# A denominator reciprocal of 128x512 turned into one of 128x128 between two trips through DRAM, with a small reordering of the setup, in a fused scan and attention kernel

## The chip, the cores and the metric

The kernel runs on one core of one Trainium2 chip. The metric is the device time of the kernel in microseconds (us); where several runs were made, the median. Lower is better. TensorE (PE) multiplies matrices, VectorE (DVE), ScalarE (ACT) and GpSimd (POOL) work elementwise, SyncE (SP) issues most of the DMAs. Each engine takes its instructions in the order in which they were written, and waits on semaphores for the others.

## The reference

Two independent branches share one output of 2048 x 1280, the first 640 columns from A and the others from B.

```python
# A: a diagonal state-space layer
Lam_bar = exp(dt * Lam);  B_bar = ((Lam_bar - 1.0) / Lam)[:, None] * Bmat
Bu = einsum("bld,pd->blp", x, B_bar)          # 2048 x 640, complex
for t in range(L): h = Lam_bar * h + Bu[:, t] # a scan along the sequence
y = 2.0 * einsum("blp,dp->bld", hseq, Cmat).real + x * Dskip
# B: attention with 32 query heads of width 20 and one shared key/value head
scores = einsum("bhqd,bkd->bhqk", q, k) * 20 ** -0.5
p = softmax(scores);  o = einsum("bhqk,bkd->bhqd", p, v) @ wo
```

The softmax divides each query's row by its denominator. The change is about how that division is prepared, and about the order of some setup work.

## The kernel before, in words

**Attention.** The 2048 queries are cut into 4 blocks of 512 (`NQB`), each block's 32 heads into 8 groups of 4 heads (`NGG`), so there are 32 groups. A group has 64 score units, one for each of its 4 heads and each of 16 chunks of 128 keys: 2048 units in all. TensorE writes the transposed scores of 3 or 2 units at a time into a PSUM tile (`R`, ring of two), and ScalarE turns the tile into exponentials in `P` (L1232, tiles of 1536 or 1024 columns in turn). About a fifth of the units goes another way: scores into a bank of `B`, then VectorE makes an approximate exponential by integer arithmetic: one pass out of PSUM (L1237, "eviction") and three shifted copies (L1242, of 1 to 3 units at once). TensorE multiplies all of them with the values and a column of ones, so that `PV` gathers, for each of 4 heads, 20 rows of output and one row of denominators. VectorE copies a finished group to `OTr` (L1275, `raw_op`), and SP stores it to DRAM, `o_rows` (`norm_ops`), 128 rows of 512 queries for each group, 32 rows for each head, with the denominators in row 20 of each 32.

**Denominators.** When all 8 groups of a block are in DRAM, `dense_ops` (L964) reads them back. Four DMAs load the block's 32 rows of denominators into `rwide`, [128, 512], the same 32 rows four times, once for each quarter of the partitions; four more load the outputs into `OTd` with head and dimension laid out densely. VectorE inverts all of `rwide` in one instruction (L982), and GpSimd multiplies `OTd` by it in 20 pieces of 128x128 (L989). Then `proj_ops` multiplies `OTd` by the output weights on TensorE. The 32 different rows of 512 denominators are thus inverted four times over. In the last block the groups 6 and 7 go another way (`norm_last`), and the dense part holds the first six, so that it can start two groups ahead of the end.

**The guard.** A bound on each query's scores is subtracted by an extra contraction row. Its weights `Md` are built in `dense_setup` by GpSimd: a memset, four selects (L600), then five multiplies (L604) with `md`, the key's largest magnitudes, which come back from DRAM (`m_row`) by four DMAs. The first matmuls that use `Md` are those of `qd_block(0)`.

**The scan (A).** `post_constants` computes small constants on GpSimd, with one reciprocal on VectorE (L709), `scan_ops` builds the output weights (`CGre`, `CGim`; GpSimd L845, VectorE L847), and for each of 4 sequence blocks and 5 channel chunks VectorE and GpSimd rotate, scan (L915) and rotate back.

**What sets the order.** `setup` is written out by hand. From then on a planner (`Plan`, `main`) writes the program when the kernel is built: it keeps a clock for each engine, takes the instruction that can begin first (with biases for each thread of work and some noise), and books it with a planned duration (`occ`) and latency (`lat`). `dve_t(n)` is n/960 + 0.07 us; a DMA is booked with at least 0.5 us of issue and 2.5 us to land. How many units go to VectorE comes out of this. `SEEDS` gives one random seed for each 64th of the score units. Each engine, SP with its DMAs too, then runs the fixed list that comes out of the plan, whatever the real durations are.

Of the kernel before, what the change touches and what calls it, by code (L numbers as in the profile page):

```python
# [9 lines left out]
ALU = mybir.AluOpType  # L10
AX = mybir.AxisListType
FP32 = mybir.dt.float32
BF16 = mybir.dt.bfloat16
# [200 lines left out]
def dve_t(n, rate=1.0):  # L214
    return n / (960.0 * rate) + 0.07
# [28 lines left out]
class _Kernel:  # L244
# [17 lines left out]


    TURNS = 64
    SEEDS = (1006, 2008, 3007, 4006, 0, 6002, 7007, 8004, 0, 10002, 11008, 0, 13008, 14008, 15009, 16002, 17007,
# [4 lines left out]

    def __init__(self, nc, t):
        self.nc, self.t = nc, t
# [21 lines left out]
    def alloc(self):  # L294
# [42 lines left out]
        self.part = self.wqd[:].rearrange("p c n -> p (c n)").bitcast(FP32)[:, 0:1280].rearrange("p (t n) -> p t n", t=2)  # L337
        self.sb("rden", [128, 2, 16], BF16)
        self.sb("rwide", [128, 512], BF16)
        self.Qs = nc.dram_tensor("q_rows", (1, 1024, 512), BF16, kind="Internal").ap()  # L340
        self.Os = nc.dram_tensor("o_rows", (self.NQB, 1024, 512), BF16, kind="Internal").ap()
        self.Ms = nc.dram_tensor("m_row", (1, 20), FP32, kind="Internal").ap()
# [236 lines left out]
    def dense_setup(self, pool):  # L579

        K, NC = self, self.NC
        go = self.go
        zero = bass.AP(tensor=K.OTr, offset=512, ap=[[1024, 32], [0, 11], [1, 512]])
        rows = lambda x, o, *ap: bass.AP(tensor=x.tensor, offset=o, ap=[*ap])
        go(self.dma(rows(K.Ms, 0, [1, 20], [1, 1]), K.mabs[0:20, 4:5], "Ms", reads=["mabs"], writes=["Ms"], kb=1))
        go(self.dma(rows(K.Qs, 21 * 512, [32 * 512, 32], [512, 11], [1, 512]), zero, "Qsz", reads=["OTr1"], writes=["Qsz"],
                    kb=352))
        last = self.NQB - 1
        for i in range(2):
            go(self.dma(K.Os[last, 128 * (6 + i):128 * (7 + i), :], K.OTr[:, 1, :], "Osz", reads=["OTr1"],  # L590
                        writes=[f"Os{last}_{6 + i}"], kb=128))
        go(self.dma(rows(K.Os, last * 1024 * 512 + (32 * 24 + 20) * 512, [32 * 512, 8], [1, 512]),
                    bass.AP(tensor=K.WO4, offset=3 * 640, ap=[[(NC + 2) * 640, 1], [0, 8], [1, 512]]), "Oso",
                    reads=["onesrow", f"Os{last}_6", f"Os{last}_7"], writes=[f"Os{last}_6", f"Os{last}_7"], kb=8))
        for dd in range(4):
            go(self.dma(K.md[32 * dd:32 * dd + 32, :], rows(K.Ms, dd, [0, 32], [4, NC]), "md", reads=["Ms"],
                        writes=[f"md{dd}"], kb=1))
        pool(lambda e: e.memset(K.Md[:], 0.0), writes=["Md"])
        for dd in range(4):
            pool(lambda e, dd=dd: e.affine_select(out=K.Md[:], in_=K.Md[:], pattern=[[0, NC], [-1, 32]],  # L600
                                                  compare_op=ALU.not_equal, fill=-1.02, base=-32 * dd, channel_multiplier=1),
                 ["Md"], ["Md"], occ=0.4)
        for m in range(NC):
            pool(lambda e, m=m: e.tensor_scalar(K.Md[:, m, :], K.Md[:, m, :], K.md[:, m:m + 1], None, op0=ALU.mult),  # L604
                 ["Md"] + [f"md{i}" for i in range(4)], ["Md"])

    def v_part(self):
        K, NC = self, self.NC
# [143 lines left out]
    def qd_block(self, qb):  # L752

        K, NC = self, self.NC
        xs = [f"xbT{c}" for c in range(NC)]
        ops, guard = [], []
        gate = lambda: self.units >= 64 * (self.NGG * (qb - 1) + 1)
        for m in range(NC):
            h = Hold()
            for c in range(NC):  # L760
                ops.append(self.mms([self.m1(lambda h=h: h.T[:, :], K.wqd[:, c, 128 * m:128 * m + 128],
                                             K.xbT[:, c, 512 * qb:512 * qb + 512], c == 0, c == NC - 1)],
                                    [f"wqd{c}"] + xs, [None], accum=c > 0, lock=c == 0, gate=gate if c == 0 else None,
                                    hold=h))
            ops.append(Op("dve", lambda e, m=m, h=h: e.tensor_scalar(K.Qd[:, m, :], h.T[:, :], self.c1, None, op0=ALU.mult),
                          [None], [f"Qd{m}"], occ=dve_t(512), free=True, hold=h))
        qd = [f"Qd{m}" for m in range(NC)]
        read = lambda: self.qread >= self.NGG * qb
        for dd in range(4):
            dst = bass.AP(tensor=K.Qs.tensor, offset=dd * 512, ap=[[32 * 512, 32], [4 * 512, NC], [1, 512]])  # L770
            ops.append(self.dma(dst, K.Qd[32 * dd:32 * dd + 32, :, :], "Qs", reads=qd, writes=[f"Qs{dd}"], kb=160,
                                gate=read if dd == 0 else None))
        h = Hold()
        seq = ["a", "a", "g", "a", "g", "a", "g", "a", "g", "g"]
        na = ng = 0
        for x in seq:
            if x == "a":
                ops.append(Op("dve", lambda e, m=na: e.tensor_scalar(
                    K.Qab[:, m % 2, :], K.Qd[:, m, :].bitcast(I16), 0x7FFF, None, op0=ALU.bitwise_and),
                    [f"Qd{na}"], [f"Qa{na % 2}", "Qpos"], occ=dve_t(512, 4), kind="fast"))  # L780
                na += 1
            else:
                ops.append(self.mms([self.m1(lambda: h.T[0:32, :], K.Md[:, ng, :], K.Qab[:, ng % 2, :].bitcast(BF16),
                                             ng == 0, ng == NC - 1, (0, 0))], ["Md", f"Qa{ng % 2}"], [None], accum=ng > 0,
                                    lock=ng == 0, hold=h))
                ng += 1
        ops.append(Op("dve", lambda e: e.tensor_copy(K.Gs[:, :], h.T[0:32, :]), [None], ["Gs"], occ=dve_t(512), free=True,
                      hold=h))
        ops.append(self.dma(bass.AP(tensor=K.Qs.tensor, offset=20 * 512, ap=[[32 * 512, 32], [1, 512]]), K.Gs[:, :], "QsG",
                            reads=["Gs"], writes=["QsG"], kb=32, done=lambda: self.qsent.add(qb)))  # L790
        return ops
# [12 lines left out]
    def scan_ops(self):  # L804
# [34 lines left out]
        for c in range(NC):  # L839
            cr, ci = K.Craw[c][:, 0, :], K.Craw[c][:, 1, :]  # L840
            keys = [f"Craw{c}0", f"Craw{c}1", "sc"] + (["ostage0", "ostage1"] if c == 4 else ws)
            for (dst, x, y, gx, gy, op, nm) in ((K.CGre, cr, ci, GRE, GIM, ALU.subtract, "CGre"),
                                                (K.CGim, ci, cr, NGRE, NGIM, ALU.add, "CGim")):
                for i in range(0, 640, 128):
                    pool(lambda e, y=y, c=c, gy=gy, i=i: e.tensor_scalar(K.ctmp[:, i:i + 128], y[:, i:i + 128], sc[:, gy, c:c + 1],  # L845
                                                                         None, op0=ALU.mult), keys, [f"ct{i}"] + ct * (i == 0), 128)
                dve(lambda e, dst=dst, x=x, op=op, c=c, gx=gx: e.scalar_tensor_tensor(  # L847
                    out=dst[:, c, :], in0=x, scalar=sc[:, gx, c:c + 1], in1=K.ctmp, op0=ALU.mult, op1=op),
                    keys + ct + [f"ct{i}" for i in range(0, 640, 128)], [nm], 640)
        sc_[-1].done = lambda: prog.update(c=1)  # L850
        for b in range(4):
            for c in range(NC):
# [110 lines left out]
    def dense_ops(self, qb):  # L963
# [4 lines left out]
        ops = []  # L968
        have = lambda: all(g in self.normed for g in range(self.NGG * qb, self.NGG * qb + (6 if qb == self.NQB - 1 else 8))) and (
            qb == 0 or qb - 1 in self.projected)  # L970
        for dd in range(4):
            src = bass.AP(tensor=K.Os.tensor, offset=base + 20 * 512, ap=[[32 * 512, 32], [1, 512]])
            ops.append(self.dma(K.rwide[32 * dd:32 * dd + 32, :], src, "rwide", reads=rd, writes=[f"rw{dd}"], kb=32,
                                gate=have if dd == 0 else None))
        for dd in range(4):
            src = bass.AP(tensor=K.Os.tensor, offset=base + dd * 512, ap=[[32 * 512, 32], [4 * 512, NC], [1, 512]])
            ops.append(self.dma(K.OTd[32 * dd:32 * dd + 32, :, :], src, "OTd", reads=rd,
                                writes=[f"OTd{m}{h}" for m in range(NC) for h in self.PIECES] if dd == 0 else [f"OTe{dd}"], kb=160))

        def recip(e):  # L980
            with self.nc.allow_low_precision("bf16 reciprocal of softmax denominator"):
                return e.reciprocal(K.rwide[:], K.rwide[:])  # L982
        rw = [f"rw{dd}" for dd in range(4)]
        ops.append(Op("dve", recip, rw, rw, occ=dve_t(512)))
        n = 512 // len(self.PIECES)
        for i, h in enumerate(self.PIECES):
            c = slice(n * i, n * i + n)
# [507 lines left out]
```

## Time and profile before

| | before |
|---|---|
| median of 3 runs (lowest to highest) | 785.59 us (785.25 to 786.33) |
| the profiled execution | 786.13 us |
| its span, first to last instruction | 784.4 us |
| ScalarE busy | 760.4 us, 97% |
| VectorE busy | 707.0 us, 90% |
| TensorE busy | 686.8 us, 88% |
| GpSimd busy | 440.8 us, 56% |

Durations and moments are those of the profiled execution, counted from the start of its span. A row of a timeline gives start, length, engine, line, operation and tiles; equal instructions that follow each other are merged, with their count behind an x, and an idle time before them stands in square brackets with what ended it. A row of a group gives line, engine, operation, count, busy time, the mean of one, and the idle time before the group with what ended it.

### The profile page before, as it was taken

The page shows a single profiled execution, that of the slowest core. Times are in us where ns is not written, and L with a number is a line of the kernel's source. Part 1 is how long each engine was busy: PE and PEld are TensorE (multiplying, and loading weights), DVE is VectorE, ACT ScalarE, POOL GpSimd, SP SyncE. Part 2 cuts the span into 40 slices and gives each one's busy share as a digit, 9 for nine tenths or more (in the row PEclk, how much of TensorE's full clock was granted, in tenths as well). Part 3 has the DMA queues.
Part 4 walks back from the last instruction along what each step waited for, and adds up shares of the span by engine and source line. Part 5 has one row for each costly group of instructions (what it writes and reads, how often), then busy time and mean ns, then how long its engine had stood idle before and what let it go on. Part 6 is the DMA issues. An engine that isn't in the chain of part 4 may idle for free.

```text
span 784.4 us, 16444 instructions
## 1 busy us (share of the span) xinstructions
PE 686.8 (88%) x6429; PEld 214.1 (27%) x6500; DVE 707.0 (90%) x1206; ACT 760.4 (97%) x688; POOL 440.8 (56%) x865
## 2 busy tenths in 40 slices
PE   5899887888879999988888999888898998889987
PEld 1222222222213233322222223222232332223333
DVE  6599899999988988899997978899999889998896
ACT  7999999999989999999998999999999999999995
POOL 4614854799987111099978300699972339990040
PEclk9799999999999999999999999999999999999999
DMA  8476101000020100220010010310002101000200
GB/s 184 86 148 124 41 15 48 16 15 15 1 55 24 39 16 16 57 58 15 14 48 25 15 39 31 65 34 16 9 23 58 37 24 39 1 14 17 65 10 34
DMA packets 59610, 31.23 MB, mean 40 GB/s; under 512 B 39942, under 2 KB 59534, under 8 KB 59534
## 3 DMA queue, kind: packets, MB, share of 16 engines
q1 hardware_dynamic: 57392, 29.86, 15.7%
q8 instruction: 52, 0.85, 0.5%
q10 hardware_dynamic: 2142, 0.32, 0.2%
q14 instruction: 24, 0.20, 0.1%
HBM read 9.08 MB, written 12.56 MB: 28 GB/s over the span
## 4 chain that ended last, share of the span: by engine, by line
ACT 68%; DVE 16%; PE 8%; POOL 2%; DMA 2%; SPq 2%; issue 1%; POOLq 0%; DVEq 0%
ACT P L1232 68%; DVE Pd L1237 5%; DVE Pd L1242 4%; PE R L418 3%; PE B L418 3%; PE PV L418 2%; DVE rwide L982 2%; DVE hh L915 1%; POOL tm L845 1%; SPq L399 1%; DMA md<-m_row 1%; DVE tm L888 1%; DMA xbT<-in_B_x_dram 1%; POOL uh L904 1%; DMA o_rows<-OTr 0%
## 5 line engine op out<-in xcount | busy, mean ns | idle before, releaser
L1232 ACT ACTIVATE P<-R 128x1536 bf16<-128x1536 f32 (+1 forms) x655 | 742.4, 1418 | 11.3 <-PE B L418 9.3
L418 PE MATMUL R<-QT,KT 32*128 32x512 bf16 (+1 forms) x1636 | 258.1, 388 | 68.3 <-ACT P L1232 47.9
L1237 DVE TENSOR_SCALAR Pd<-B 128x512 int16<-128x512 f32 x412 | 278.4, 682 | 32.2 <-PE B L418 28.4
L1242 DVE TENSOR_SCALAR Pd<-Pd 128x1536 int16<-128x1536 int16 (+2 forms) x501 | 256.8, 546 | 1.2
L418 PE MATMUL PV<-Pd,VP 128*32 128x512 bf16 x1648 | 251.1, 385 | 2.6 <-DVE OTr L1275 1.2
L418 PE MATMUL PV<-P,VP 128*32 128x512 bf16 x1636 | 248.8, 387 | 3.2 <-DVE Pd L1242 2.7
L904 POOL TENSOR_TENSOR tm<-hh,cs 128x128 bf16<-128x128 f32 x320 | 165.6, 540 | 22.9 <-DVE hh L915 10.1
L418 PE MATMUL B<-QT,KT 32*128 32x512 bf16 x412 | 159.5, 387 | 0.0
L418 PEld LDWEIGHTS R<-QT,KT 32*128 32x128 bf16 (+1 forms) x1636 | 64.2, 91 | 305.9 <-ACT P L1232 274.5
L904 POOL TENSOR_TENSOR W<-tm 128x128 bf16<-128x128 bf16 x160 | 89.7, 583 | 97.5 <-PE B L418 93.4
L904 POOL TENSOR_TENSOR uh<-tm 128x128 bf16<-128x128 bf16 x160 | 82.1, 534 | 81.8 <-DVE tm L888 77.4
L418 PEld LDWEIGHTS PV<-Pd,VP 128*32 128x32 bf16 x1648 | 59.5, 94 | 66.4 <-issue 40.9
L418 PEld LDWEIGHTS PV<-P,VP 128*32 128x32 bf16 x1636 | 57.5, 94 | 60.2 <-issue 42.3
L989 POOL TENSOR_TENSOR OTd<-OTd,rwide 128x128 bf16<-128x128 bf16 x80 | 32.7, 436 | 51.4 <-DVE rwide L982 49.5
L888 DVE TENSOR_TENSOR tm<-B,cs 128x1024 bf16<-128x1024 f32 x40 | 48.6, 1214 | 1.7 <-PE B L418 1.2
L418 PE MATMUL B<-CGre,W 128*128 128x384 bf16 (+1 forms) x160 | 46.5, 305 | 0.1
L418 PE MATMUL B<-CGim,W 128*128 128x384 bf16 (+1 forms) x160 | 45.6, 299 | 0.0
L915 DVE TENSOR_TENSOR_SCAN hh<-sc,hini,uh 128x512 f32<-128x512 f32 x30 | 40.4, 1345 | 0.0
L845 POOL TENSOR_SCALAR tm<-W,sc 128x128 f32<-128x128 bf16 x40 | 31.6, 802 | 14.7 <-DVE CGre L847 8.1
L418 PEld LDWEIGHTS B<-QT,KT 32*128 32x128 bf16 x412 | 37.3, 91 | 0.0
L418 PE MATMUL B<-xaT,BTre 128*128 128x512 bf16 x89 | 27.2, 383 | 2.1 <-issue 1.3
L418 PE MATMUL B<-xaT,BTim 128*128 128x512 bf16 x85 | 27.1, 392 | 2.2 <-issue 1.7
(149 smaller groups left out, 416.5 us busy)
## 6 DMA issues: line engine op xcount, KB each, us to landing
o_rows<-OTr SPq DMA_DIRECT2D x32, 128.0 KB, 1.7
QT<-q_rows SPq DMA_DIRECT2D x30, 128.0 KB, 2.2
q_rows<-Qd SPq DMA_DIRECT2D x16, 160.0 KB, 2.8
OTd<-o_rows SPq DMA_DIRECT2D x16, 160.0 KB, 3.4
out_dram<-ystage SPq DMA_DIRECT2D x16, 160.0 KB, 1.8
out_dram<-ostage SPq DMA_DIRECT2D x12, 160.0 KB, 1.8
P<-in_B_wq_dram SPq DMA_DIRECT2D x1, 800.0 KB, 5.4
WO<-in_B_wo_dram SPq DMA_DIRECT2D x4, 200.0 KB, 3.6
```

Source lines behind the costliest of these rows:

```text
L399: return e.dma_start_transpose(out_ap, in_ap)
L418: ins = e.matmul(o() if callable(o) else o, lhsT=l, rhs=r, start=st, stop=sp, skip_group_check=True, **kw)
L845: pool(lambda e, y=y, c=c, gy=gy, i=i: e.tensor_scalar(K.ctmp[:, i:i + 128], y[:, i:i + 128], sc[:, gy, c:c + 1], None, op0=ALU.mult), key ...
L888: dve(lambda e, k=k, h=h: e.tensor_tensor(K.tm[:, 2 * k:2 * k + 2, :], bass.AP(tensor=K.BB, offset=512 * int(h.key[1]), ap=[[512 * self.BA ...
L904: put(lambda e, c0=c0, end=end: e.tensor_tensor(out[:, c0:end], a[:, c0:end], b[:, c0:end], op), reads, [writes + h], n, gate=None if i el ...
L915: dve(lambda e, ri=ri, ini=ini: e.tensor_tensor_scan(K.hh[:, ri, :], dec, K.uh[:, ri, :], ini, ALU.mult, ALU.add), ["sc", *(f"uh{ri}{h}" f ...
L982: return e.reciprocal(K.rwide[:], K.rwide[:])
L989: ops.append(Op("pool", lambda e, c=c, m=m: e.tensor_tensor(K.OTd[:, m, c], K.OTd[:, m, c], K.rwide[:, c], ALU.mult), rw + [f"OTe{dd}" for ...
L1232: return Op("act", lambda e: e.activation(dst, K.R[n % 2][:, 0:512 * size], ACT.Exp, scale=self.exp_scale), [f"R{n % 2}"] + ["R0c"] * (siz ...
L1237: return Op("dve", lambda e: e.tensor_scalar(K.Pd[:, 0, u, :], K.B[x][:, :], self.d_off, 0.0, op0=ALU.add, op1=ALU.max), [f"B{x}"], [f"Pd{ ...
L1242: return Op("dve", lambda e: e.tensor_scalar(K.Pd[:, i, a:b, :], K.Pd[:, 0, a:b, :], float(self.SHIFTS[i]), 0.0, op0=ALU.subtract, op1=ALU ...
```

## The change

The diff has five parts.

1. `dense_ops`: the block's denominators are loaded into a new buffer `rblk`, [128, 128], in four DMAs of 32 rows by 128 columns, so that each denominator is there once, the four column quarters stacked on the partitions. VectorE inverts `rblk` in one instruction. Four DMAs write it back over the denominators in `o_rows`, and four DMAs load the inverted rows into `rwide`, four times over as before. For each block there are 8 more DMAs, all in SP's queue, and `rwide` waits for the stores. GpSimd's multiplies are unchanged, and now wait for the loads of `rwide` where they waited for VectorE.
2. The five multiplies that finish `Md` move from `dense_setup` to `qd_block(0)`, so that the planner places them; they come behind the scan's constants on GpSimd.
3. The planned latency of the `md` DMAs is 5.5 in place of 2.5.
4. The planned duration of the `CGre` and `CGim` instructions is that of 695 columns in place of 640.
5. The seeds are others, so the planner's order differs on every engine.

```diff
@@ -262,11 +262,10 @@
     TURNS = 64
-    SEEDS = (1006, 2008, 3007, 4006, 0, 6002, 7007, 8004, 0, 10002, 11008, 0, 13008, 14008, 15009, 16002, 17007,
...
+    SEEDS = (1006, 2007, 3008, 4004, 5008, 6003, 0, 8008, 9006, 0, 11003, 0, 13002, 14008, 0, 16002, 17003,
...
@@ -337,6 +336,7 @@
         self.part = self.wqd[:].rearrange("p c n -> p (c n)").bitcast(FP32)[:, 0:1280].rearrange("p (t n) -> p t n", t=2)
         self.sb("rden", [128, 2, 16], BF16)
         self.sb("rwide", [128, 512], BF16)
+        self.sb("rblk", [128, 128], BF16)
         self.Qs = nc.dram_tensor("q_rows", (1, 1024, 512), BF16, kind="Internal").ap()
         self.Os = nc.dram_tensor("o_rows", (self.NQB, 1024, 512), BF16, kind="Internal").ap()
         self.Ms = nc.dram_tensor("m_row", (1, 20), FP32, kind="Internal").ap()
@@ -593,16 +593,15 @@
                     bass.AP(tensor=K.WO4, offset=3 * 640, ap=[[(NC + 2) * 640, 1], [0, 8], [1, 512]]), "Oso",
                     reads=["onesrow", f"Os{last}_6", f"Os{last}_7"], writes=[f"Os{last}_6", f"Os{last}_7"], kb=8))
         for dd in range(4):
-            go(self.dma(K.md[32 * dd:32 * dd + 32, :], rows(K.Ms, dd, [0, 32], [4, NC]), "md", reads=["Ms"],
-                        writes=[f"md{dd}"], kb=1))
+            o = self.dma(K.md[32 * dd:32 * dd + 32, :], rows(K.Ms, dd, [0, 32], [4, NC]), "md", reads=["Ms"],
+                         writes=[f"md{dd}"], kb=1)
+            o.lat = 5.5
+            go(o)
         pool(lambda e: e.memset(K.Md[:], 0.0), writes=["Md"])
         for dd in range(4):
             pool(lambda e, dd=dd: e.affine_select(out=K.Md[:], in_=K.Md[:], pattern=[[0, NC], [-1, 32]],
                                                   compare_op=ALU.not_equal, fill=-1.02, base=-32 * dd, channel_multiplier=1),
                  ["Md"], ["Md"], occ=0.4)
-        for m in range(NC):
-            pool(lambda e, m=m: e.tensor_scalar(K.Md[:, m, :], K.Md[:, m, :], K.md[:, m:m + 1], None, op0=ALU.mult),
-                 ["Md"] + [f"md{i}" for i in range(4)], ["Md"])
 
     def v_part(self):
         K, NC = self, self.NC
@@ -771,6 +770,9 @@
             ops.append(self.dma(dst, K.Qd[32 * dd:32 * dd + 32, :, :], "Qs", reads=qd, writes=[f"Qs{dd}"], kb=160,
                                 gate=read if dd == 0 else None))
         h = Hold()
+        if qb == 0:
+            ops.extend(Op("pool", lambda e, m=m: e.tensor_scalar(K.Md[:, m, :], K.Md[:, m, :], K.md[:, m:m + 1], None, op0=ALU.mult),
+                          ["Md"] + [f"md{i}" for i in range(4)], ["Md"], occ=0.25) for m in range(NC))
         seq = ["a", "a", "g", "a", "g", "a", "g", "a", "g", "g"]
         na = ng = 0
         for x in seq:
@@ -846,7 +848,7 @@
                                                                          None, op0=ALU.mult), keys, [f"ct{i}"] + ct * (i == 0), 128)
                 dve(lambda e, dst=dst, x=x, op=op, c=c, gx=gx: e.scalar_tensor_tensor(
                     out=dst[:, c, :], in0=x, scalar=sc[:, gx, c:c + 1], in1=K.ctmp, op0=ALU.mult, op1=op),
-                    keys + ct + [f"ct{i}" for i in range(0, 640, 128)], [nm], 640)
+                    keys + ct + [f"ct{i}" for i in range(0, 640, 128)], [nm], 695)
         sc_[-1].done = lambda: prog.update(c=1)
         for b in range(4):
             for c in range(NC):
@@ -968,20 +970,29 @@
         ops = []
         have = lambda: all(g in self.normed for g in range(self.NGG * qb, self.NGG * qb + (6 if qb == self.NQB - 1 else 8))) and (
             qb == 0 or qb - 1 in self.projected)
+        row = base + 20 * 512
+        den = lambda b: bass.AP(tensor=K.Os.tensor, offset=row + 128 * b, ap=[[32 * 512, 32], [1, 128]])
+        part = lambda b: K.rblk[32 * b:32 * b + 32, :]
+        rb = [f"rb{b}" for b in range(4)]
+
+        def recip(e):
+            with self.nc.allow_low_precision("bf16 reciprocal of softmax denominator"):
+                return e.reciprocal(K.rblk[:], K.rblk[:])
+        for b in range(4):
+            ops.append(self.dma(part(b), den(b), "rblk", reads=rd, writes=[rb[b]], kb=8, gate=have if b == 0 else None))
+        ops.append(Op("dve", recip, rb, rb, occ=0.85))
+        for b in range(4):
+            ops.append(self.dma(den(b), part(b), "rrow", reads=[rb[b]], writes=[f"rr{qb}{b}"], kb=8))
+        rw = [f"rw{dd}" for dd in range(4)]
         for dd in range(4):
-            src = bass.AP(tensor=K.Os.tensor, offset=base + 20 * 512, ap=[[32 * 512, 32], [1, 512]])
-            ops.append(self.dma(K.rwide[32 * dd:32 * dd + 32, :], src, "rwide", reads=rd, writes=[f"rw{dd}"], kb=32,
-                                gate=have if dd == 0 else None))
+            src = bass.AP(tensor=K.Os.tensor, offset=row, ap=[[32 * 512, 32], [1, 512]])
+            ops.append(self.dma(K.rwide[32 * dd:32 * dd + 32, :], src, "rwide", reads=[f"rr{qb}{b}" for b in range(4)],
+                                writes=[rw[dd]], kb=32))
         for dd in range(4):
             src = bass.AP(tensor=K.Os.tensor, offset=base + dd * 512, ap=[[32 * 512, 32], [4 * 512, NC], [1, 512]])
             ops.append(self.dma(K.OTd[32 * dd:32 * dd + 32, :, :], src, "OTd", reads=rd,
                                 writes=[f"OTd{m}{h}" for m in range(NC) for h in self.PIECES] if dd == 0 else [f"OTe{dd}"], kb=160))
 
-        def recip(e):
-            with self.nc.allow_low_precision("bf16 reciprocal of softmax denominator"):
-                return e.reciprocal(K.rwide[:], K.rwide[:])
-        rw = [f"rw{dd}" for dd in range(4)]
-        ops.append(Op("dve", recip, rw, rw, occ=dve_t(512)))
         n = 512 // len(self.PIECES)
         for i, h in enumerate(self.PIECES):
             c = slice(n * i, n * i + n)
```

In the program that comes out, 417 units go to VectorE (412 before) and 1631 to ScalarE (1636 before).

7 rows, old and new, of the table SEEDS are left out of this document.

## The prediction

> **What bounds the kernel now.** I read the page's engine shares first, then the groups of instructions, then ScalarE's timeline for its gaps, and last the other engines around each gap.
>
> ```profile
> PE 686.8 (88%) x6429; PEld 214.1 (27%) x6500; DVE 707.0 (90%) x1206; ACT 760.4 (97%) x688; POOL 440.8 (56%) x865
> ...
> L1232 ACT ACTIVATE P<-R 128x1536 bf16<-128x1536 f32 (+1 forms) x655 | 742.4, 1418 | 11.3 <-PE B L418 9.3
> ```
>
> ScalarE is the bound: its exponentials (L1232) alone take 742.4 us. The kernel's time is what lies before the first of them, their sum, the gaps between them, and a tail. Its timeline, merged, starts a new row at each gap and puts the gap in brackets:
>
> ```profile
> 21.87 11.47 ACT L1232 ACTIVATE P<-R 128x1536 bf16<-128x1536 f32 x10 [0.42 <-PE R L418]
> 34.12 2.37 ACT L1232 ACTIVATE P<-R 128x1536 bf16<-128x1536 f32 x2 [0.78 <-PE PV L418]
> 36.67 2.37 ACT L1232 ACTIVATE P<-R 128x1536 bf16<-128x1536 f32 x2 [0.18 <-PE R L418]
> 39.94 4.63 ACT L1232 ACTIVATE P<-R 128x1536 bf16<-128x1536 f32 x4 [0.91 <-PE B L418]
> 44.81 43.69 ACT L1232 ACTIVATE P<-R 128x1536 bf16<-128x1536 f32 x38 [0.25 <-PE B L418]
> 88.66 16.07 ACT L1232 ACTIVATE P<-R 128x1536 bf16<-128x1536 f32 x14 [0.16 <-PE R L418]
> 104.99 64.73 ACT L1232 ACTIVATE P<-R 128x1536 bf16<-128x1536 f32 x57 [0.25 <-PE B L418]
> 169.96 57.52 ACT L1232 ACTIVATE P<-R 128x1024 bf16<-128x1024 f32 x51 [0.24 <-PE B L418]
> 229.22 2.37 ACT L1232 ACTIVATE P<-R 128x1536 bf16<-128x1536 f32 x2 [1.74 <-PE B L418]
> 232.01 184.68 ACT L1232 ACTIVATE P<-R 128x1536 bf16<-128x1536 f32 x163 [0.42 <-PE B L418]
> 418.03 1.02 ACT L1232 ACTIVATE P<-R 128x1024 bf16<-128x1024 f32 x1 [1.35 <-PE B L418]
> 420.53 13.76 ACT L1232 ACTIVATE P<-R 128x1536 bf16<-128x1536 f32 x12 [1.47 <-PE B L418]
> 434.48 171.30 ACT L1232 ACTIVATE P<-R 128x1536 bf16<-128x1536 f32 x151 [0.19 <-PE B L418]
> 606.65 1.02 ACT L1232 ACTIVATE P<-R 128x1024 bf16<-128x1024 f32 x1 [0.87 <-PE B L418]
> 608.07 140.42 ACT L1232 ACTIVATE P<-R 128x1536 bf16<-128x1536 f32 x124 [0.40 <-PE B L418]
> 749.69 25.45 ACT L1232 ACTIVATE P<-R 128x1536 bf16<-128x1536 f32 x23 [1.20 <-PE B L418]
> ```
>
> Nearly all gaps fall in four places, at 229, 418, 607 and 750: 1.74 + 0.42 + 1.35 + 1.47 + 0.19 + 0.87 + 0.40 + 1.20 = **7.64 us**. The five up to 44.81 make 2.54, the other three 0.65. What stands ahead of each of the four places on VectorE (the timeline by engine; the PE row is from the first place, and the last two rows are busy time by stretch: length, PE, PE loads, DVE, ACT, POOL, granted clock, DMA share, GB/s):
>
> ```profile
> 224.06 3.34 DVE L982 RECIPROCAL rwide<-rwide 128x512 bf16<-128x512 bf16 x1
> ...
> 228.44 0.39 PE L418 MATMUL PV<-P,VP 128*32 128x512 bf16 x1 [2.44 <-DVE Pd L1242]
> 413.62 3.34 DVE L982 RECIPROCAL rwide<-rwide 128x512 bf16<-128x512 bf16 x1
> 601.85 3.35 DVE L982 RECIPROCAL rwide<-rwide 128x512 bf16<-128x512 bf16 x1
> 745.35 3.34 DVE L982 RECIPROCAL rwide<-rwide 128x512 bf16<-128x512 bf16 x1
> 229.22:232.01 2.79, 2.46 (x20) 0.58 (x21) 1.39 (x3) 2.37 (x3) 2.56 (x8) 0.59 0.00 0
> 417.00:421.00 4.00, 3.28 (x15) 0.76 (x16) 2.00 (x4) 1.50 (x2) 3.66 (x10) 0.57 0.23 78
> ```
>
> Each place is one reciprocal. VectorE runs in order, so a shift (L1242) or an eviction (L1237) queued behind the reciprocal comes late; TensorE, in order too, waits for it (2.44 us at 228.44) with the next score matmuls behind; ScalarE runs dry. The planner books this reciprocal at 512/960 + 0.07 = 0.60 us; it takes 3.34. So each block runs 2.74 us behind its plan, four blocks 10.96, of which 7.64 reach ScalarE (0.70). The last two rows show a second loss: after the stall TensorE's granted clock is 0.59 and 0.57.
>
> **The change part by part.** *The reciprocal.* Four of 512 columns become four of 128; this width is not in the trace, so it is bounded by its neighbours, the narrow ones and the wide one above:
>
> ```profile
> L1004 DVE RECIPROCAL rden<-B 128x16 bf16<-128x16 f32 x2 | 0.5, 252 | 0.6 <-PE B L418 0.6
> 37.99 0.19 DVE L709 RECIPROCAL sc<-sc 128x5 f32<-128x5 f32 x1 [1.83 <-POOL sc L698]
> L1237 DVE TENSOR_SCALAR Pd<-B 128x512 int16<-128x512 f32 x412 | 278.4, 682 | 32.2 <-PE B L418 28.4
> L1242 DVE TENSOR_SCALAR Pd<-Pd 128x1536 int16<-128x1536 int16 x315 | 190.2, 631 | 0.5
> L1242 DVE TENSOR_SCALAR Pd<-Pd 128x512 int16<-128x512 int16 x81 | 23.9, 331 | 0.2
> ```
>
> 0.19 us at 5 columns and 3.34 at 512 make 6.2 ns a column, so 0.19 + 123 x 6.2 ns = 0.95 us. The ends are 0.25 (16 columns) and 3.34. I take 0.95, nearest to the line through three rows. The plan now books 0.85: the misfit falls from 2.74 to 0.10 us, VectorE saves 4 x 2.39 = 9.6 us, and the 7.64 us should go almost whole. I leave 1.5 us of it in, since the changeover of a block also brings projections and stores. If all goes, 0; if none, 7.64.
>
> The Trainium skill, "VectorE: DVE Perf Modes", section "Walkthrough: the 8-slice pipeline in each mode", says that the reciprocal is an iterative divide with a repeat count of 8. An estimate from that page's 0.96 GHz is 8.3 ns a column, 4.3 us for 512, where the trace has 3.34; the measurement decides. By the page 128 columns would take 1.1 us and the sum would be about half a microsecond worse.
>
> *The new plan.* The instruction lists of both programs differ in the split: 417 score units on VectorE in place of 412, 1631 in place of 1636 on ScalarE (325 exponentials of 1536 and 328 of 1024, against 327, 327 and one of 512). The row at 232.01 gives 184.68/163 = 1.133 us for one, 2.5 units each: 0.453 us a unit. Five units less are **2.3 us** off the bound. VectorE pays 5 x 278.4/412 = 3.4 us, and for 24 more single shifts and 3 fewer triple ones (24 x 23.9/81 - 3 x 190.2/315) 5.3 us: 8.7 us that the 9.6 saved cover. Without that cover they would come onto a VectorE that is 90% busy. TensorE gets 15 more PV matmuls net and 20 fewer idle-filling ones, about nothing.
>
> *The guard's weights.* GpSimd waited 5.22 us for `md` and came to the scan's constants behind it:
>
> ```profile
> 26.74 1.80 POOL L600 TENSOR_SCALAR_AFFINE_SELECT Md<-Md 128x160 bf16<-128x160 bf16 x4
> 33.77 2.21 POOL L604 TENSOR_SCALAR Md<-Md,md 128x32 bf16<-128x32 bf16 x5 [5.22 <-DMA md<-m_row]
> ```
>
> In the new order the constants follow L600 at 28.5 and not at 35.9, 7.4 us earlier; the five multiplies come behind them at about 36, when `md` has long landed (33.8), so that wait is gone and none takes its place. VectorE's reciprocal of the constants, which waited 1.83 us (the row at 37.99), comes loose, and the 0.91 us gap at 39.94 stands behind it. From 0 to 0.91; I take **0.5**.
>
> *Two more trips.* SP issues 32 more transfers, and each block's chain grows:
>
> ```profile
> 737.68 1.73 SPq L401 DMA_DIRECT2D rwide<-o_rows  x4
> 739.45 1.86 SPq L401 DMA_DIRECT2D OTd<-o_rows  x4
> QT<-q_rows SPq DMA_DIRECT2D x30, 128.0 KB, 2.2
> OTd<-o_rows SPq DMA_DIRECT2D x16, 160.0 KB, 3.4
> rwide<-o_rows SPq DMA_DIRECT2D x16, 32.0 KB, 1.8
> md<-m_row SPq DMA_DIRECT2D x4, 0.6 KB, 5.0
> DMA to landing us min/median/max: 3.1/5.0/6.3
> 748.83 8.65 POOL L989 TENSOR_TENSOR OTd<-OTd,rwide 128x128 bf16<-128x128 bf16 x20 [42.33 <-DVE rwide L982]
> ```
>
> (The landing range is `md`'s.) A pass of four small transfers is 1.73 us of issue and 1.8 to land. SP held 3.6 us per block (1.73 + 1.86); with its waits for the reciprocal and the stores it will hold 1.73 + 1.8 + 0.95 + 1.73 + 1.8 + 3.6 = 11.6. Behind it stand the `QT` loads and the `o_rows` stores, 8 us later: a load's gate opens two groups ahead, and a group is 64 of 2048 units in 754 us, 23.6 us, so this is hidden. In blocks 0 to 2 the projection has a whole block to wait. The last block counts: by the lists its reciprocal lies at 70 ScalarE units left, its first projection at 23, so 47 x 0.453 = 21.3 us lie between. Needed: 0.95, then 1.73 + 1.8 back, then 1.73 + 1.86 + 3.4 until `OTd` has landed, then 15 of GpSimd's 20 multiplies, 6.5: 18.0 us. It is covered by 3.3 us; beyond that each microsecond is one of the end. I take 0.
>
> The Trainium skill, "DMA: Bandwidth & Descriptors", section "Specifications", says that transfers below 512 B make the DMA engine read, modify and write; the new blocks have rows of 256 B. No run here shows that size; by the page these trips would take longer than `rwide`'s. That speaks against the change and is the second rival's mechanism.
>
> Wider booked costs of L847 and of `md` change only the plan. The tail (from 749.69 + 25.45 = 775.1 to the span's end at 784.4, 9.3 us) has the same instructions in both lists.
>
> *Sum*, from the profiled execution's 786.13: - (7.64 - 1.5) - 2.3 - 0.5 = -8.9, so 777.2; it ran 0.54 us above the median shown, 785.59, from which the sum gives 776.7. I say **777.0**.
>
> **The rivals.** *VectorE becomes the bound.* The 8.7 us of extra units and shifts are real work, while the saving sits in four places. For it: VectorE is 90% busy over the span. Against: its total falls by 0.9 us. If half of them come out on ScalarE, 777.0 + 4.4 = 781.4; if all, 785.7, no change.
>
> *The first trip is late (the slower side).* The narrow reciprocal stands in VectorE's queue and waits for four loads that the plan lets land in 2.5 us. If short rows land like `md`'s (up to 6.3 us) and not like `rwide`'s (1.8), VectorE stands 3.8 us in each block: 4 x 3.8 x 0.70 = 10.6 us of gaps. In the last block the way back and `OTd` are late by 4.5 + 2.9 less the 3.3 of cover, 4.1. So 786.13 - 7.64 - 2.3 - 0.5 + 10.6 + 4.1 = 790.4. It turns slower from a landing of about 5.4 us. Against: `md` ran among the loads of the start.
>
> *The gaps belong to the changeover*, to the projections and stores there, not to the reciprocal. Then only 2.3 goes: 783.5. Against: the 2.44 us wait at 228.44, for a shift right behind the reciprocal.
>
> *The change doesn't do what it says*: the narrow reciprocal costs as much as the wide. The gaps stay and 8.7 us of VectorE work come on top, at 0.70: 786.13 - 2.3 + 6.1 = 789.9. The 252 ns row speaks against it.
>
> **How the numbers follow.** Forecast 0.72; VectorE half bound 0.09, wholly 0.04; late trip 0.06; changeover 0.06; no shorter 0.03. A measurement of this kernel can tell 0.2% (1.6 us) from no change. Faster holds the forecast, the half bound and the changeover: 0.87; same 0.04; slower 0.09. The range goes from all gaps of the four places and the early 2.54 gone (785.59 - 7.64 - 2.3 - 2.5 = 773.1) to the changeover case, 783.5.
>
> **What would show it.** Four reciprocals of about 0.95 us; no gap over 0.5 us on ScalarE behind them and a granted clock near 1.00 there; 653 exponentials with a sum near 740; GpSimd without the 5.22 us wait; small `rblk` landings below 2.5 us; the first projection of the last block without a wait. A reciprocal above 2 us, landings of 5 us, or new gaps in other places would make the prediction wrong.

## The result, and the profile after

The changed kernel takes 775.17 us (median of 4 runs, 773.65 to 776.14) against 785.96 us for the kernel before (4 runs, one more than above): a ratio of 0.9861, 95% interval 0.9842 to 0.988. That is 10.8 us less; the forecast was 777.0, with a range of 773.1 to 783.5. The profiled execution takes 775.14 us, its span 773.2 us (786.13 and 784.4 before).

Engine shares and ScalarE's group in the page of the changed kernel (the exponentials now stand in L1243; the last column is the gaps before them):

```profile
PE 697.5 (90%) x6495; PEld 213.1 (28%) x6495; DVE 702.4 (91%) x1232; ACT 757.0 (98%) x686; POOL 441.0 (57%) x865
...
L1243 ACT ACTIVATE P<-R 128x1536 bf16<-128x1536 f32 (+1 forms) x653 | 739.2, 1421 | 3.3 <-PE B L418 1.1
```

ScalarE's timeline of the changed kernel, with a row for each gap:

```profile
21.54 11.63 ACT L1243 ACTIVATE P<-R 128x1536 bf16<-128x1536 f32 x10 [0.42 <-PE R L418]
33.79 324.79 ACT L1243 ACTIVATE P<-R 128x1536 bf16<-128x1536 f32 x286 [0.62 <-PE PV L418]
359.28 2.37 ACT L1243 ACTIVATE P<-R 128x1536 bf16<-128x1536 f32 x2 [0.69 <-PE B L418]
361.88 18.44 ACT L1243 ACTIVATE P<-R 128x1536 bf16<-128x1536 f32 x16 [0.24 <-PE B L418]
380.50 187.69 ACT L1243 ACTIVATE P<-R 128x1536 bf16<-128x1536 f32 x166 [0.18 <-PE B L418]
568.62 195.02 ACT L1243 ACTIVATE P<-R 128x1536 bf16<-128x1536 f32 x173 [0.43 <-PE R L418]
```

Sixteen rows have become six. The four places behind the reciprocals are gone altogether: these now start at 222, 412, 594 and 730, and no row begins behind them. TensorE's granted clock is 1.00 over the 10 us from the start of each; before, it fell to 0.59 and 0.57 behind the first two stalls, and was 1.00 at the other two (606 to 609 and 749 to 752).

By the group's last column the gaps fell from 11.3 to 3.3 us (8.0): 7.6 at the four places and 1.5 up to 45 us (2.54 to 1.04), while the others grew by 1.1, with new ones at 359 to 381 and at 569. The exponentials fell from 742.4 to 739.2 (3.2). The first exponential starts 0.33 us earlier, and the tail is 9.6 us (763.64 to 773.2) and not 9.3. Together that is the 11 us.

The reciprocal, the transfers around it and the last block's chain (tile view and timelines of the changed kernel; the landing range is that of `rblk`, both ways):

```profile
L980 DVE RECIPROCAL rblk<-rblk x4: 937/942/943, 222.1 to 730.5; 128x128 bf16<-128x128 bf16 x4
DMA to landing us min/median/max: 1.4/1.6/2.6
731.47 1.70 SPq L401 DMA_DIRECT2D o_rows<-rblk  x4
734.25 1.69 SPq L401 DMA_DIRECT2D rwide<-o_rows  x4
735.99 2.85 SPq L401 DMA_DIRECT2D OTd<-o_rows  x4
741.60 8.91 POOL L1000 TENSOR_TENSOR OTd<-OTd,rwide 128x128 bf16<-128x128 bf16 x20 [55.44 <-DMA OTd<-o_rows]
751.64 0.45 PE L418 MATMUL B<-WO,OTd 128*128 128x320 bf16 x2
```

The narrow reciprocal takes 0.942 us. One landing took 2.6 us, just above the 2.5 of the forecast's sign; VectorE waited for none. The first projection of the last block needs fifteen of the twenty multiplies; by an estimate of three quarters of their 8.91 us these end at 741.60 + 6.68 = 748.3, and it starts at 751.64: 3.4 us of cover.

At the start, GpSimd comes to the guard's weights without a wait:

```profile
30.29 0.19 DVE L708 RECIPROCAL sc<-sc 128x5 f32<-128x5 f32 x1 [1.74 <-POOL sc L697]
34.89 2.23 POOL L774 TENSOR_SCALAR Md<-Md,md 128x32 bf16<-128x32 bf16 x5
```

VectorE still waits 1.74 us for the constants, but at 30 us, where its next instruction waits 2.20 us more for TensorE anyway, and no longer at 38.

### The profile page after: what moved, and what is told of

Its sections match the earlier page's. It is cut to its first block, busy times and chain, and to the rows that moved or that the text cites. A ratio compares the mean times of both kernels' runs of the same rounds, so it can differ in the third digit from the quotient of the medians.

```text
span 773.2 us, 16569 instructions
## 1 busy us (share of the span) xinstructions
PE 697.5 (90%) x6495; PEld 213.1 (28%) x6495; DVE 702.4 (91%) x1232; ACT 757.0 (98%) x686; POOL 441.0 (57%) x865
## 4 chain that ended last, share of the span: by engine, by line
ACT 69%; POOL 10%; DVE 10%; PE 8%; SPq 1%; issue 1%; DMA 1%; DVEq 0%; POOLq 0%
ACT P L1243 69%; POOL tm L906 4%; DVE Pd L1253 4%; POOL W L906 3%; PE R L418 3%; DVE Pd L1248 3%; PE PV L418 3%; PE B L418 2%; POOL uh L906 2%; SPq L399 1%; DVE hh L917 1%; DVE tm L890 1%; DMA xbT<-in_B_x_dram 1%; POOL tm L847 0%; DVE mabs L529 0%
## 5 line engine op out<-in xcount | busy, mean ns | idle before, releaser
L1243 ACT ACTIVATE P<-R 128x1536 bf16<-128x1536 f32 (+1 forms) x653 | 739.2, 1421 | 3.3 <-PE B L418 1.1
L1248 DVE TENSOR_SCALAR Pd<-B 128x512 int16<-128x512 f32 x417 | 282.3, 683 | 32.3 <-PE B L418 29.2
L1253 DVE TENSOR_SCALAR Pd<-Pd 128x1536 int16<-128x1536 int16 (+2 forms) x522 | 259.9, 530 | 1.2
L418 PE MATMUL PV<-P,VP 128*32 128x512 bf16 x1631 | 256.2, 389 | 0.8 <-DVE Pd L1248 0.4
L418 PE MATMUL B<-QT,KT 32*128 32x512 bf16 x417 | 161.6, 388 | 0.0
L906 POOL TENSOR_TENSOR W<-tm 128x128 bf16<-128x128 bf16 x160 | 91.9, 597 | 89.8 <-PE B L418 85.9
L418 PEld LDWEIGHTS PV<-P,VP 128*32 128x32 bf16 x1631 | 59.2, 94 | 61.0 <-issue 45.9
L847 POOL TENSOR_SCALAR tm<-W,sc 128x128 f32<-128x128 bf16 x40 | 30.7, 779 | 20.0 <-DVE CGre L849 12.5
L418 PE MATMUL B<-xaT,BTim 128*128 128x512 bf16 x100 | 30.4, 384 | 0.6 <-DVE tm L890 0.4
L418 PE MATMUL PV<-cs,VP 128*128 128x512 bf16 x88 | 30.5, 390 | 0.0
```

The source lines that it names most:

```text
L418: ins = e.matmul(o() if callable(o) else o, lhsT=l, rhs=r, start=st, stop=sp, skip_group_check=True, **kw)
L906: put(lambda e, c0=c0, end=end: e.tensor_tensor(out[:, c0:end], a[:, c0:end], b[:, c0:end], op), reads, [writes + h], n, gate=None if i el ...
L1243: return Op("act", lambda e: e.activation(dst, K.R[n % 2][:, 0:512 * size], ACT.Exp, scale=self.exp_scale), [f"R{n % 2}"] + ["R0c"] * (siz ...
L1248: return Op("dve", lambda e: e.tensor_scalar(K.Pd[:, 0, u, :], K.B[x][:, :], self.d_off, 0.0, op0=ALU.add, op1=ALU.max), [f"B{x}"], [f"Pd{ ...
L1253: return Op("dve", lambda e: e.tensor_scalar(K.Pd[:, i, a:b, :], K.Pd[:, 0, a:b, :], float(self.SHIFTS[i]), 0.0, op0=ALU.subtract, op1=ALU ...
```

## The experiments

The theory was that the length of one VectorE instruction in each block made the gaps. The rivals: that they belong to the changeover of a block; that the planner's wrong booking and not the length made them; and that the gain is that of the new order. Six of the kernels keep every engine's list of instructions as it was (those named with `fixed` or `trips`), so that a plan made anew can't blur them. Ratios are to the kernel before, run in the same comparison.

### The kernel before with a narrow reciprocal (narrow_fixed)

```diff
-                return e.reciprocal(K.rwide[:], K.rwide[:])
+                return e.reciprocal(K.rwide[:, 0:128], K.rwide[:, 0:128])
```

> The kernel before with the list of every engine unchanged; only the reciprocal of each block inverts columns 0 to 127 of rwide and leaves out the other 384 (so three quarters of the denominators are not inverted). My theory, that the length of this one instruction makes the four groups of gaps: four reciprocals of 0.95 us in place of 3.34, the 7.64 us of gaps on ScalarE at the four places fall to under 1.5, still 655 exponentials, 778.4 to 779.9 us in place of 786. Rival, the gaps belong to the changeover of a block: gaps stay at 6 to 8 us, 785 to 786 us.

Measured: 776.58 us against 786.43, ratio 0.9879 (0.9865 to 0.9894). From its groups and ScalarE's timeline:

```profile
L982 DVE RECIPROCAL rwide<-rwide 128x128 bf16<-128x128 bf16 x4 | 3.8, 940 | 0.0
...
L1232 ACT ACTIVATE P<-R 128x1536 bf16<-128x1536 f32 (+1 forms) x655 | 741.5, 1437 | 3.1 <-PE B L418 1.8 <-PE PV L418 0.5 <-PE R L418 0.2
...
168.65 258.83 ACT L1232 ACTIVATE P<-R 128x1024 bf16<-128x1024 f32 x229 [0.24 <-PE B L418]
427.66 337.87 ACT L1232 ACTIVATE P<-R 128x1536 bf16<-128x1536 f32 x299 [0.19 <-PE B L418]
```

From 168.65 to the last exponential ScalarE stops once, for 0.19 us. With nothing else changed, 4 x 2.40 us less on VectorE take about 9.5 us off the kernel by the ratio. In the profiles the gaps fall by 8.2 (11.3 to 3.1), 7.45 of it at the four places, and the same 655 exponentials by 0.9, 742.4 to 741.5. The first exponential also starts 0.76 us earlier, 200 us before the first reciprocal; in the profiles of this case it starts between 21.1 and 23.0 us. The changeover is refuted. The theory holds, and its size was too small by two to three microseconds: the time lies below the 778.4 to 779.9 expected.

### The changed kernel with a wide reciprocal (wide_fixed)

```diff
-                return e.reciprocal(K.rblk[:], K.rblk[:])
+                return e.reciprocal(K.OTp[:, 1, :].rearrange("p (b n) -> p b n", b=4),
+                                    bass.AP(tensor=K.rblk, offset=0, ap=[[128, 128], [0, 4], [1, 128]]))
...
-            ops.append(self.dma(den(b), part(b), "rrow", reads=[rb[b]], writes=[f"rr{qb}{b}"], kb=8))
+            ops.append(self.dma(den(b), K.OTp[32 * b:32 * b + 32, 1, 0:128], "rrow", reads=[rb[b]], writes=[f"rr{qb}{b}"], kb=8))
```

> The changed kernel with the list of every engine unchanged; the reciprocal of each block reads rblk four times over and writes 512 columns, of which 128 are used. My theory: four reciprocals of about 3.3 us, 2.4 longer each, and with 0.70 us of gap for each us that VectorE is late, 6.7 us of gaps come back behind the four reciprocals: 775.2 + 6.7 = 781.9 us. Rival, the gain comes from the new order and its seeds: within 1 us of 775.2. Rival, the gaps come in full: 775.2 + 9.6 = 784.8 us.

Measured: 783.08 us, ratio 0.996 (0.9946 to 0.9974); the reciprocals take 3.34 us. ScalarE's group, and the rows of its timeline behind the first and the last reciprocal:

```profile
L1244 ACT ACTIVATE P<-R 128x1536 bf16<-128x1536 f32 (+1 forms) x653 | 740.2, 1400 | 9.2 <-PE B L418 6.3 <-PE R L418 1.8 <-PE PV L418 0.5
...
226.42 3.43 ACT L1244 ACTIVATE P<-R 128x1024 bf16<-128x1024 f32 x3 [0.80 <-PE B L418]
230.32 2.37 ACT L1244 ACTIVATE P<-R 128x1536 bf16<-128x1536 f32 x2 [0.47 <-PE B L418]
...
739.62 2.36 ACT L1244 ACTIVATE P<-R 128x1536 bf16<-128x1536 f32 x2 [1.22 <-PE B L418]
742.72 27.71 ACT L1244 ACTIVATE P<-R 128x1536 bf16<-128x1536 f32 x25 [0.73 <-PE B L418]
```

The gaps come back in their places, 6.6 us behind the four reciprocals (9.2 in all in place of 3.3), and 1.0 us more for the same 653 exponentials. By the ratios the wide reciprocal costs 0.996 - 0.9861 = 0.0099, 7.8 us, give or take 1.9. That refutes the first rival; it lies between the 6.7 of the theory and the 9.6 of the other rival and can't decide between them. The new order and its seeds don't make the wide reciprocal harmless.

### The changed kernel with the old seeds (after_oldseeds)

The edit puts the old `SEEDS` into the changed kernel; the planner makes another order.

> The changed kernel with the seeds of the kernel before; the planner makes another order and gives VectorE 399 units in place of 417, ScalarE 1649. My theory, that ScalarE's units are the sum's largest term and the narrow reciprocal still leaves no gaps: 18 x 0.453 = 8.2 us more, 783.4 us, reciprocals without a gap over 0.5 us behind them. Rival, the seeds shuffle the order and the number of units doesn't set the time: 775 to 778 us. Rival, the old seeds bring gaps of their own besides: over 786 us.

Measured: 787.72 us, ratio 1.0018 (1.0006 to 1.003): 0.2% above the kernel before, and 12.5 above the changed kernel. Its groups on ScalarE and VectorE:

```profile
L1244 ACT ACTIVATE P<-R 128x1536 bf16<-128x1536 f32 (+1 forms) x660 | 747.7, 1403 | 5.2 <-PE B L419 2.4 <-PE PV L419 1.2 <-PE R L419 0.8
L1249 DVE TENSOR_SCALAR Pd<-B 128x512 int16<-128x512 f32 x399 | 271.2, 683 | 48.3 <-PE B L419 44.9
```

The exponentials take 8.5 us more than in the changed kernel, which is the 18 units (8.2). The gaps are 5.2 us and not 3.3, none of them behind a reciprocal: the largest, 1.22 us, begins at 741.50, before the last reciprocal at 741.98. The start is 0.84 us later and the tail 0.3 longer; this makes the 11.5 us by which the span (784.7) is longer than that of the changed kernel. So the third theory is nearest: most of it is units, with gaps, start and tail besides. The seeds belong to the plan for which they were chosen: the same diff without its line of seeds would have looked like a change that does nothing.

### The kernel before with the reciprocal booked at its length (before_truth, truth_seeds)

```diff
-        ops.append(Op("dve", recip, rw, rw, occ=dve_t(512)))
+        ops.append(Op("dve", recip, rw, rw, occ=3.35))
```

> The kernel before, reciprocal unchanged (3.34 us), but booked by the planner at 3.35 us in place of 0.60; its seeds are the old ones, the order is another, and VectorE gets 389 units in place of 412. Theory that the gaps come from the booking: the four groups of gaps go (7.6 us) while 23 units more on ScalarE cost 23 x 0.453 = 10.4 us: 788 to 789 us. Theory that the length makes gaps whatever the plan knows: the gaps stay, 786 + 10.4 = 796 us. Theory that the number of units doesn't count: 778 us.

Measured: 793.77 us, ratio 1.0106 (1.0071 to 1.014). This is inconclusive: in the profiled execution, the slowest of the four at 798.33, the gaps right behind the reciprocals went, but gaps of about the same sum came at other places (2.03 us at 631, 1.46 at 771), and the median lies between the two theories. As in after_oldseeds, seeds chosen for another plan spoil the comparison, so the same booking was run with seeds searched for it, nine at each turn:

> The kernel before with its reciprocal of 3.34 us booked at 3.35 and seeds searched for that plan (nine to choose from at each of the 64 turns, by the planner's own end). VectorE gets 396 units, 16 less than before and 21 less than in the changed kernel; ScalarE 1652. Theory that a known length makes no gaps but takes VectorE's time from the units: gaps of 7.6 us go, 16 x 0.453 = 7.2 us come, 785 to 787 us. Theory that booking it right is all the change needed: 776 to 779 us. Theory that the length makes gaps whatever the plan knows: 792 to 794 us.

Measured: 785.52 us, ratio 1.0 (0.9987 to 1.0013). Its groups:

```profile
L1228 ACT ACTIVATE P<-R 128x1024 bf16<-128x1024 f32 (+1 forms) x661 | 749.1, 1414 | 4.1 <-PE B L414 2.9 <-PE R L414 0.4
L1233 DVE TENSOR_SCALAR Pd<-B 128x512 int16<-128x512 f32 x396 | 268.9, 684 | 49.6 <-PE B L414 46.4
```

A plan that knows the length makes no gaps (4.1 us in all) and pays in units: 396 on VectorE, 749.1 us of exponentials. The 9.6 us of VectorE time cost about the same either way (785.52 us with the booking right, 786.57 with it wrong); only a shorter instruction gets them back. So the length is the cause of the loss, and the booking only chose its form, gaps or units.

### The guard's weights without their wait, old order (md_fixed)

```diff
-            pool(lambda e, m=m: e.tensor_scalar(K.Md[:, m, :], K.Md[:, m, :], K.md[:, m:m + 1], None, op0=ALU.mult),
+            pool(lambda e, m=m: e.tensor_scalar(K.Md[:, m, :], K.Md[:, m, :], K.half_pi[:, 0:1], None, op0=ALU.mult),
                  ["Md"] + [f"md{i}" for i in range(4)], ["Md"])
+            waits, fn, sem = self.p.ops["pool"][-1]
+            self.p.ops["pool"][-1] = ([w for w in waits if w[0] != "md"], fn, sem)
```

> The kernel before with the list of every engine unchanged; GpSimd's five multiplies of the guard's weights take a constant in place of md and so don't wait for its four DMAs (the guard's weights are thus wrong, and the factor md is left out). My theory: the 5.2 us wait of GpSimd and the 1.8 us wait of VectorE for the scan's constants go, and the 0.91 us gap of ScalarE near 40 us goes with them: 0.5 to 0.9 us less than the kernel before, 785.5. Rival, the early gaps come from TensorE's own first matmuls: gaps near 34 to 45 us add up to 2 us as before, no change. Rival, constants that come 5 us earlier pull in more than the gap: over 1.5 us less.

Measured: 785.17 us against 786.57, ratio 0.9991 (0.9975 to 1.0007), which can't be told from no change. Its trace says more (ScalarE's timeline up to 88 us, GpSimd's row at 28):

```profile
22.96 11.48 ACT L1234 ACTIVATE P<-R 128x1536 bf16<-128x1536 f32 x10 [0.41 <-PE R L418]
34.66 52.54 ACT L1234 ACTIVATE P<-R 128x1536 bf16<-128x1536 f32 x46 [0.22 <-PE PV L418]
...
28.49 2.23 POOL L604 TENSOR_SCALAR Md<-Md,half_pi 128x32 bf16<-128x32 bf16 x5
```

The four gaps at 34 to 45 us, 0.78 + 0.18 + 0.91 + 0.25 before, are one of 0.22: 1.9 us, more than the one gap that the theory named. In this execution the first exponential starts 1.09 us later than before, which hides part of it; even so the 56th ends 1.3 us earlier (87.20 against 88.50). So the wait made these gaps, as far as one execution of each can show; what the median gains lies inside its interval.

### The trips in smaller pieces (slow_trips, trips_32B, trips_8B)

In these, the four column blocks of `rblk` take interleaved columns, so that each DMA moves the same bytes in more pieces: single elements of 2 bytes, or runs of 32 or 8 bytes, in place of rows of 256.

```diff
-        den = lambda b: bass.AP(tensor=K.Os.tensor, offset=row + 128 * b, ap=[[32 * 512, 32], [1, 128]])
+        den = lambda b: bass.AP(tensor=K.Os.tensor, offset=row + b, ap=[[32 * 512, 32], [4, 128]])
```

> The changed kernel with the list of every engine unchanged; the loads and stores of rblk take every fourth column, so each moves single elements of 2 bytes and lands late. By the second rival's formula of the prediction, for a landing of L us in place of 1.7: four times 0.70 x (L - 2.5) of gaps behind the narrow reciprocal, and in the last block twice (L - 1.6) less 3.3 of cover at the end; L = 6 gives 9.8 + 5.5, 790 us, L = 4 gives 4.2 + 1.5, 781 us. Theory that VectorE has slack enough to wait and only the last block counts: 775.2 + 5.5 at L = 6, 781 us, and no gaps behind the first three reciprocals. Theory that all of it is hidden: 775 us.

Measured: 1483.01 us, ratio 1.8852 (1.8774 to 1.893); none of the three theories was near. SP's timeline in the first block, ScalarE's two largest gaps there, and from the waits of the whole run VectorE's for the loads of `rblk` (in all, times, longest):

```profile
213.89 14.37 SPq L401 DMA_DIRECT2D rblk<-o_rows  x4
237.49 102.14 SPq L401 DMA_DIRECT2D o_rows<-rblk  x4
409.79 1.72 SPq L401 DMA_DIRECT2D rwide<-o_rows  x4
...
239.73 1.02 ACT L1243 ACTIVATE P<-R 128x1024 bf16<-128x1024 f32 x1 [14.82 <-PE B L418]
421.46 1.02 ACT L1243 ACTIVATE P<-R 128x1024 bf16<-128x1024 f32 x1 [158.36 <-PE R L418]
...
DVE rblk L980 <- DMA rblk<-o_rows: 62.2, 4, 17.2
```

The store pass took 172 us (237.49 to 409.79), far past any cover, so the time itself says nothing of a trip that is a little late. The loads say more. VectorE stood 62.2 us for them in four waits, and ScalarE had a gap behind each, of 14.82, 13.25, 14.32 and 16.37 us: 58.8 in all, 0.94 us of gap for each us of waiting. Two milder ones followed, with runs of 16 and 4 elements (`[[32 * 512, 32], [64, 8], [1, 16]]` and `[[32 * 512, 32], [16, 32], [1, 4]]`, `rblk` viewed to match).

> The changed kernel with the list of every engine unchanged; the loads and stores of rblk move runs of 32 bytes in place of rows of 256, eight times as many pieces. With single elements (slow_trips) a store pass of 16384 pieces took about 172 us and a load pass 22 us, where the changed kernel takes 2.8 and about 3.3: per piece that makes 10.5 and 1.4 ns, so 1024 pieces about 10.8 and 3.3 us. Theory that the trips are hidden but for the last block's cover of 3.3 us: the store pass 8 us longer, QT loads behind it 8 us later and still hidden, the end 8.0 - 3.3 = 4.7 us later: 775.2 + 4.7 = 779.9 us, no new gaps in the first three blocks. Rival, SP's queue has no slack: gaps also in blocks 0 to 2, over 785 us. Rival, the landing doesn't depend on the pieces at this size: 775 us.

Measured: 774.04 us, ratio 0.9852 (0.9823 to 0.9881): as the changed kernel. The last rival holds; the transfers became hardly slower (a store pass takes 3.2 us in the first block and 3.0 in the last, where it took 2.8; `rblk` of trips_32B, both ways, and its two rows in the DMA view, us to landing at the end):

```profile
DMA to landing us min/median/max: 1.5/1.7/2.4
rblk<-o_rows SPq DMA_DIRECT2D x16, 8.0 KB, 1.8
o_rows<-rblk SPq DMA_DIRECT2D x16, 8.0 KB, 1.7
```

> As trips_32B, with runs of 8 bytes: 4096 pieces a pass, by the same figures a store pass of about 43 us and a load pass of about 5.6. Theory that the trips are hidden but for the last block and the loads that the reciprocal waits for: the end about 40 - 3.3 = 37 us later, and the loads 2.3 us later than in the changed kernel in four blocks, 4 x 0.70 x 2.3 = 6.4 us of gaps: about 819 us; the QT loads 40 us later are just on time, two groups being 46 us. Rival, SP's queue has no slack of that size: gaps of tens of us in the first three blocks where TensorE waits for QT, over 840 us.

Measured: 869.84 us, one run: far above the 819 of the theory, and past the 840 of the rival, though not for the rival's reason. SP's timeline in block 0, ScalarE's largest gap in each of blocks 0 to 2, and from the waits what stood behind two of them:

```profile
223.07 2.92 SPq L401 DMA_DIRECT2D o_rows<-rblk  x4
252.69 1.72 SPq L401 DMA_DIRECT2D rwide<-o_rows  x4
...
263.60 1.02 ACT L1243 ACTIVATE P<-R 128x1024 bf16<-128x1024 f32 x1 [17.58 <-PE R L418]
468.46 1.02 ACT L1243 ACTIVATE P<-R 128x1024 bf16<-128x1024 f32 x1 [22.93 <-PE B L418]
675.51 2.53 ACT L1243 ACTIVATE P<-R 128x1536 bf16<-128x1536 f32 x2 [20.88 <-PE B L418]
...
PE B L418 <- POOL OTd L1000: 27.2, 2, 17.3
DVE ystage L951 <- DMA out_dram<-ystage: 44.8, 2, 23.3
```

The store pass of block 0 took 29.6 us where it takes 2.8 in the changed kernel, 26.8 later. In block 0 TensorE stood 17.3 us for the projection; in blocks 1 and 2 VectorE stood for the store of `ystage`, issued behind the pieces and landing late, with the next copy into that single buffer held up. The store passes of blocks 1 and 2 were 26.9 and 27.9 us longer than in the changed kernel. Taking from each the gap that it made, 17.6, 22.9 and 20.9, leaves an estimated cover of about 9, 4 and 7 us. In the changed kernel block 0's can also be read off: the first projection needs five of the twenty multiplies, which end at about 235.3 (a quarter of their 8.79 us from 233.05 on), and it starts at 242.69, 7.4 us later. No row shows TensorE waiting for `QT`. In the last block the store pass was 26.7 us longer and the gaps from 805 us on are 22.7, close to 26.7 less the 3.4 of cover. Of these TensorE's wait for the projection is 10.0; what made the rest the trace doesn't show.

## Why the prediction was right, point by point

- *The bound and the cause.* Right, and shown from both sides: narrow_fixed takes the gaps away from the old order, wide_fixed puts them back into the new one. The second loss, the clock, was there in two of the four places only.
- *The size of the reciprocal's term.* Mis-sized: 6.1 us forecast, about 9.5 measured at a fixed order (ratio interval: 8.3 to 10.6 us). The 1.5 us left in for the changeover was not needed, since at a fixed order one gap of 0.19 us remained there; and gaps were counted by their own lengths, though the same 655 exponentials are 0.9 us shorter in sum without them. That makes 8.5; the rest of the 9.5 lies within the interval. The instruction's own duration, 0.942 us against 0.95 forecast, was right.
- *The page's rule on the reciprocal.* The estimate of 1.1 us worked out from the Trainium skill, "VectorE: DVE Perf Modes", section "Walkthrough: the 8-slice pipeline in each mode", lies above the 0.942 us of the trace.
- *The new plan.* 2.3 us forecast. The exponentials fell by 3.2, of which 0.9 came without any change of units in narrow_fixed, so 2.3 are left if the two simply add up. The 1.1 us of new gaps in the new order were not in the forecast. Nor does the term show how much hangs on the seeds: with seeds chosen for another plan the changed kernel is 12.5 us slower (787.72 against 775.17), more than the whole gain.
- *The guard's weights.* 0.5 us forecast; by the trace up to 1.9 us of gaps went with the wait (md_fixed) and 1.5 in the changed kernel, by the median of md_fixed the time changes by -2 to +0.6 us. The cause was right, the size remains open. VectorE's own wait did not go, as the forecast had it; it came earlier, where it cost nothing.
- *The trips.* Nothing forecast, and the last block's cover of 3.3 us was 3.4. Right there. Wrong in the working for blocks 0 to 2: the forecast named the `QT` loads and a whole block of time for the projection, and trips_8B showed about 4 to 9 us of cover, set by the projection's place in TensorE's list and by the stores of `ystage`. The trips of the changed kernel never used it up.
- *The second rival.* It was kept for short rows that land late. In the changed kernel the four loads land in 1.7 us, no later than `rwide`'s rows of 1024 B (1.9), and even runs of 32 bytes did so in 1.8. The Trainium skill's limit of 512 B, "DMA: Bandwidth & Descriptors", section "Specifications", brings no later landing at this size. The rival's mechanism is real where loads land late enough: in slow_trips they landed in 13.0 us and VectorE stood for them. But with 8-byte runs they landed in 3.6 us and VectorE still didn't wait, so the 2.5 us from which the rival counted was too early. The price that I set, 0.70 us of gap for each us of lateness, came out as 0.94 there (58.8 of 62.2 us), and as 0.69 for the longer reciprocals of wide_fixed (6.6 of 9.6).
- *The sum.* 8.9 us forecast, 10.8 measured. The reciprocal's term alone was 3.4 us too small, more than the difference of 1.9. The rest of the change had 2.8 us in the forecast; by the ratios of narrow_fixed and of the changed kernel it brings 0.9879 - 0.9861 = 0.0018, 1.4 us, give or take 1.9, which can't be told from nothing. So the two misses partly cancel, and that the sum came so near is in part luck. How the rest divides between the guard, the units and the new order's own gaps can't be settled at such intervals.

## What to carry to other kernels

When one engine is nearly full, list its gaps one by one and look at what stood on the in-order engines just ahead of each; four of VectorE's 1206 instructions made most of them. In this kernel a planner that books an instruction too short turns it into gaps, and one that books it right gives up other work; only making it shorter gains. When a plan is made anew, compare plans that are equally well searched, and test the cause at a fixed order.

## What the runs showed of the hardware that I had not expected

- VectorE's reciprocal takes 0.252 us at 16 columns, 0.942 at 128 and 3.34 at 512 (fp32 out of PSUM at 16, bf16 out of SBUF at the others): 6.2 ns a column, whether the source is read once or, in wide_fixed, four times over.
- A DMA of 8 KB in 256 runs of 32 bytes lands as soon as one in 32 rows of 256 (1.7 to 1.8 us against 1.5 to 1.7). At runs of 8 bytes a store pass of four took 29.6 us, at single elements 172 us, 7.2 and 10.5 ns a piece; the loads were far quicker: one of 8-byte runs lands in 3.6 us, one of single elements in 13.0.
- A transfer issued behind such stores lands late although its own instruction was issued at once: in trips_8B VectorE waited up to 23.3 us for a store of `ystage`.
